# A long convolution by a two-stage transform: the spectral product as three real products, formed per k1 from PSUM and written in place

## Chip, cores, metric

The kernel runs on one core of one Trainium2 chip. The metric is the device time of one execution in microseconds (us). Engines: PE (TensorE) with its weight loads (PEld), DVE (VectorE), ACT (ScalarE), POOL (GpSimd), SP (SyncE, which issues most DMAs).

## What is computed

```python
def _A_ref(q, k, v, shift_k, ssm_k, ssm_D):          # S = 2048, D = 512
    ...
    for t in range(ks):                              # ks = 4
        k_shift = k_shift + k_pad[:, t:t + S, :] * shift_k[:, ks - 1 - t][None, None, :]
    kv = k_shift * v
    ...                                              # transforms of length 2S of kv and ssm_k, zero padded
    y_f = kv_f * kf_f[None, :, :, :]
    y = irfft(y_f)[:S]
    y = y + kv * ssm_D[None, None, :]
    return q * y
...
h = x + _A_ref(_layernorm(x, axis=-1), A_k, A_v, A_shift_k, A_ssm_k, A_ssm_D)
h2 = h + relu(_layernorm(h, axis=-1) @ w1) @ w2      # Dff = 1376
```

All inputs and the output are bf16. The lines on the transform are shortened here: y is the causal convolution of kv with ssm_k along the 2048 tokens, channel by channel.

## The kernel before

The convolution is computed by matmuls at odd frequencies, each transform split in two stages: 32 values k1 by 64, over n1 (32) and n2 (64) tokens. The program is written in an order by hand and kept in it: each engine runs its instructions in the order of the source, and waits only where data, a tile's buffer or a PSUM bank calls for it. The stages, in order:

1. **Loads and tables.** `sk` (ssm_k), then k and v transposed by DMA, on SP's queue. DVE and POOL make turn tables, ACT makes sines of them: f1hi and f1lo for stage 1, cc, cs, cn (`table`, L183; negation on POOL, L204) for stage 2, each with the sine doubled to two halves of 64 columns.
2. **Rows of ssm_k** (`to_rows`, L220): 64 PE transposes of bf16 128x128, eight copies of 128x1024 out of PSUM, in turn by DVE and ACT.
3. **Stage 1 of ssm_k and the taps** (loop at L281): per group gb, `stage1` is 64 matmuls of 32 rows, four row groups at a time, into two PSUM tiles of two banks, each emptied by one copy (L213 on ACT, L215 on DVE) to a1k. `taps` (L272) makes half a chunk of k_shift by eight matmuls of 512 columns, and DVE multiplies it with vT (L279). PSUM: four buffers of two banks.
4. **Rows of kv** (L291), then **stage 2 of ssm_k** (L298): 128 matmuls of 256 columns; DVE writes the real part plus ssm_D to kf, ACT the imaginary part.
5. **Stage 1 of kv** (L311) to a1x.
6. **Product** (L328 and L346, loop at L364): per pair of k1, eight stage 2 matmuls of kv to the tiles u; ACT copies 80 of 256 columns to usb for POOL; DVE and POOL form all four real products (L341); two pairs later PE adds them by ipos and ineg (four matmuls of 512 columns, L351), and ACT copies the sums over kf. The loads of x (first half) and w1 start in this loop.
7. **Inverse stage 1** (`inv1`, L474): per batch of four groups eight matmuls of 256 columns with kf as weights and dre, dim moving, then one copy of 128x1024 to ax. Between the batches stand the layernorm of x, the tables ecore (ec_turns on POOL, ec_wrap on DVE, ec_sins on ACT; two work buffers ecw), and the centring of w1.
8. **Inverse stage 2, gate and MLP** (`inv2`, `gate`, `mlp1`, `mlp2`) over four quarters of the tokens; output by DMA.

Of the kernel before, what the change touches and what calls it, by code (L numbers as in the profile page):

```python
# [9 lines left out]
ALU = mybir.AluOpType  # L10
# [5 lines left out]
P = 128  # L16
# [40 lines left out]
def kernel(  # L57
# [28 lines left out]
    slotA = pl.push("slotA")  # L86
    vp = pl.push("vp")
    early = pl.push("early")
    wp = pl.push("wp", side="right")
    kvp = pl.push("kvp", side="right")  # L90
    psum = pl.push("psF", bufs=4, space=PSUM)


    sk = early.tile([P, DC, S], BF16, name="sk")
    nc.sync.dma_start(out=sk[:], in_=A_ssm_k.rearrange("(c p) t -> p c t", p=P))
    wsh = consts.tile([P, DC, KS], BF16, name="wsh")
    nc.scalar.dma_start(out=wsh[:], in_=A_shift_k.rearrange("(r p) j -> p r j", p=P))
    dtab = consts.tile([P, 64, DC], BF16, name="dtab")
    draw = consts.tile([P, DC, 64], BF16, name="draw")
    for dp in range(2):  # L100
        src = bass.AP(tensor=A_ssm_D.tensor, offset=A_ssm_D.offset + 64 * dp, ap=[[0, 64], [P, DC], [1, 64]])
        nc.scalar.dma_start(out=draw[64 * dp:64 * dp + 64, :, :], in_=src)
    vT = vp.tile([P, DC, S], BF16, name="vT")
    CH = 512
    kT = [(kvp if c < 2 else early).tile([P, DC, CH + 16], BF16, name=f"kT{c}") for c in range(4)]
    wdiag = kvp.tile([P, DC, KS, P], BF16, name="wdiag")
# [9 lines left out]

# [5 lines left out]
    eps_t = consts.tile([P, 1], F32, name="eps_t")  # L122
    nc.vector.memset(eps_t[:], EPS)

    hsc = consts.tile([P, 2], F32, name="hsc")
    hbi = consts.tile([P, 2], F32, name="hbi")
    for t_, v_ in ((hsc, TURN / 8192), (hbi, -0.5 * TURN)):
        nc.vector.memset(t_[:], 0.0)
        for dp in range(2):
            nc.vector.memset(t_[halves[dp], dp:dp + 1], v_)  # L130
# [6 lines left out]
    n1i = early.tile([P, 1], I32, name="n1i")  # L137
    for s in range(0, P, 32):
        nc.gpsimd.iota(n1i[s:s + 32, :], pattern=[[0, 1]], base=0, channel_multiplier=1)
    r1 = early.tile([P, 32], I32, name="f1_r")  # L140
    nc.gpsimd.iota(r1[:], pattern=[[2, 32]], base=1, channel_multiplier=0)
    n2i = early.tile([P, 1], I32, name="n2i")
    for s in range(0, P, 64):
        nc.gpsimd.iota(n2i[s:s + 64, :], pattern=[[0, 1]], base=0, channel_multiplier=1)
    r2 = early.tile([P, 32, 64], I32, name="w_r")
    nc.gpsimd.iota(r2[:], pattern=[[2, 32], [128, 64]], base=1, channel_multiplier=0)
    r3 = early.tile([P, 64], I32, name="dm_r")
    nc.gpsimd.iota(r3[:], pattern=[[1, 64]], base=0, channel_multiplier=0)
    ident = consts.tile([P, P], BF16, name="ident")
    nc.gpsimd.memset(ident[:], 0.0)  # L150
    nc.gpsimd.affine_select(out=ident[:], in_=ident[:], compare_op=ALU.not_equal, fill=1.0,
                            base=0, pattern=[[-1, P]], channel_multiplier=1)

    n1c = early.tile([P, 1], F32, name="n1c")
    n2c = early.tile([P, 1], F32, name="n2c")
# [3 lines left out]
    t1 = early.tile([P, 64], I32, name="f1_t")  # L159
    _turns(nc, t1[:, 0:32], r1[:], n1c[:], 128, True)  # L160
    _turns(nc, t1[:, 32:64], r1[:], n1c[:], 128, False)
    f1f = early.tile([P, 64], F32, name="f1_f")
# [4 lines left out]
    def pieces(name, *sizes):  # L167
        got, at = [], 0
        for i, n in enumerate(sizes):
            got.append((at, wp.tile([P, n, P], F32R, tag=f"{name}{i}", name=f"{name}{i}")))  # L170
            at += n
        return got

    cc, cs, cn = pieces("c2c", 16, 16), pieces("c2s", 22, 10), pieces("c2n", 8, 8, 8, 8)

    def at_k1(tab, k1):
        a, t = [p for p in tab if p[0] <= k1][-1]
        return t[:, k1 - a, :]

    tsn = early.tile([P, 32, 64], I32, name="w_ts")  # L180
    _turns(nc, tsn[:], r2[:], n2c[:], 8192, False)

    def table(dst, turns):  # L183
        for a, t in dst:
            for dp in range(2):
                nc.scalar.activation(out=t[:, :, 64 * dp:64 * dp + 64], in_=turns[:, a:a + t.shape[1], :], func=ACT.Sin,  # L186
                                     scale=hsc[:, dp:dp + 1], bias=hbi[:, dp:dp + 1])

    table(cs, tsn)
    f1hi = consts.tile([P, P], BF16, name="f1_hi")  # L190
    f1lo = consts.tile([P, P], BF16, name="f1_lo")
    for f in (f1hi, f1lo):
        nc.gpsimd.memset(f[:, 64:128], 0.0)
    nc.vector.tensor_copy(out=f1hi[:, 0:64], in_=f1f[:])
    f1d = early.tile([P, 64], F32, name="f1_d")
    nc.vector.tensor_tensor(out=f1d[:], in0=f1f[:], in1=f1hi[:, 0:64], op=ALU.subtract)
    nc.vector.tensor_copy(out=f1lo[:, 0:64], in_=f1d[:])
    _turns(nc, r2[:], r2[:], n2c[:], 8192, True)
# [3 lines left out]
    for a, b in ((0, 8), (8, 16), (16, 22), (22, 24), (24, 32)):  # L202
        (ao, to), (ai, ti) = [[p for p in tab if p[0] <= a][-1] for tab in (cn, cs)]
        nc.gpsimd.tensor_single_scalar(out=to[:, a - ao:b - ao, :], in_=ti[:, a - ai:b - ai, :].bitcast(F32), scalar=-1.0,  # L204
                                       op=ALU.mult)


    nc.gpsimd.tensor_copy(out=dtab[:], in_=draw[:].rearrange("p r g -> p g r"))

# [7 lines left out]
    def bank2(name):  # L217
        return psum.tile([P, 2, 512], F32, tag="ps", name=name)

    def to_rows(src, q, fl, eng):  # L220
        pst = psum.tile([P, 2, 8, P], BF16, tag="ps", name="pst")
        for i in range(8):
            nc.tensor.transpose(out=pst[:, 0, i, :], in_=src[:, :, :, 8 * q + i], identity=ident[:])  # L223
        copy(eng, fl[:, :, :, 8 * q:8 * q + 8], pst[:, 0, :, :].rearrange("p i (d g) -> p g d i", d=2))

    def stage1(fl, a_out, gb, engs, wide=False):

        pss = [bank2("ps1") for _ in range(2)]
        outs = [pss[rg // 2][:, rg % 2, :] for rg in range(4)]
        for gi in range(8):  # L230
            for f, first in ((f1hi, True), (f1lo, False)):
                for rg in range(4):
                    rows = slice(32 * rg, 32 * rg + 32)
                    w = 128 if wide and gi < 7 else 64
                    nc.tensor.matmul(out=outs[rg][:, 64 * gi:64 * gi + w],  # L235
                                     lhsT=fl[rows, 8 * gb + gi, :, :].rearrange("p d n -> p (d n)"),
                                     rhs=f[rows, 0:w], start=first, stop=not first,
                                     tile_position=(32 * rg, 0), skip_group_check=True)
        for h in range(2):
            copy(engs[h], a_out[:, :, 32 * gb:32 * gb + 32].rearrange("p c (g r) -> p c g r", r=DC)[:, :, :, 2 * h:2 * h + 2],  # L240
                 pss[h][:].rearrange("p r (g c) -> p c g r", c=64))

    def stage2(ps, a_in, kp, s):

        for kk in range(2):
            k1 = 2 * kp + kk
            w_re, w_im = ((cc, cs), (cn, cc))[s]
            nc.tensor.matmul(out=ps[:, kk, :], lhsT=at_k1(w_re, k1), rhs=a_in[:, k1, :], start=True, stop=False,  # L248
                             skip_group_check=True)
            nc.tensor.matmul(out=ps[:, kk, :], lhsT=at_k1(w_im, k1), rhs=a_in[:, 32 + k1, :], start=False, stop=True,  # L250
                             skip_group_check=True)
# [393 lines left out]
```

## Time and profile before

| | us |
|---|---|
| median of 3 runs | 229.88 |
| lowest, highest | 229.82, 231.06 |
| span of the profiled execution, first to last instruction | 230.8 |

The span of the profiled execution is 0.9 us above the median of the runs, and inside their lowest and highest.

| engine | busy us | share of the span |
|---|---|---|
| PE | 201.4 | 87% |
| PEld | 142.4 | 62% |
| DVE | 142.9 | 62% |
| ACT | 118.1 | 51% |
| POOL | 78.3 | 34% |

A line of the groups gives the source line, the engine, the operation, what it writes from what, the shape written and read, and the count; then busy us, mean ns of one; then the idle time of that engine before it and what ended it. A line of the waits reads "who, on which line <- for whom: us in total, times, longest". A line by stretch gives the busy us of PE, PEld, DVE, ACT and POOL with their counts, then the granted share of PE's clock, the DMA share and GB/s. Matmuls are pipelined, so the duration of one is longer than the distance between the starts of two.

### The profile page before, as it was taken

The numbers are of one execution on the slowest core, as the hardware profiler recorded it, in microseconds if no ns is written. First come the engines' busy times: TensorE is split into PE (matmuls) and PEld (weight loads), VectorE is DVE, ScalarE is ACT, GpSimd is POOL, SyncE is SP. The second block draws the span as 40 slices with busy tenths as digits, with TensorE's granted clock in tenths as the row PEclk, the third lists the DMA queues.
The fourth block names the chain that finished last, engine by engine and source line by source line (L and its number), as shares of the span: only waits on it lengthen the run. The fifth ranks groups of instructions, "written<-read, shape, count | busy, mean of one in ns | idle before, by whom it ended". The sixth has DMA issues, their size and how long they took to land.

```text
span 230.8 us, 5978 instructions
## 1 busy us (share of the span) xinstructions
PE 201.4 (87%) x2544; PEld 142.4 (62%) x2544; DVE 142.9 (62%) x214; ACT 118.1 (51%) x177; POOL 78.3 (34%) x108
## 2 busy tenths in 40 slices
PE   0485999899966699999898889999999999999991
PEld 0473454899955699998787775444744474444440
DVE  7974667676664589998685869583971346134031
ACT  3789766555585478888486501750162026206400
POOL 6399910000000599998860770400220002002000
PEclk9999999999999589999999997999999999999998
DMA  6999920000000000772962168977244214021011
GB/s 197 306 230 161 169 60 3 0 4 0 0 7 6 3 1 0 182 244 77 211 119 53 33 214 127 213 140 114 54 91 96 55 37 91 6 59 27 3 46 46
DMA packets 49194, 20.10 MB, mean 87 GB/s; under 512 B 44208, under 2 KB 47632, under 8 KB 49168
## 3 DMA queue, kind: packets, MB, share of 16 engines
q1 hardware_dynamic: 46688, 18.24, 37.7%
q10 hardware_dynamic: 2480, 1.48, 2.4%
q8 instruction: 20, 0.33, 0.6%
q14 instruction: 6, 0.05, 0.1%
HBM read 7.08 MB, written 2.10 MB: 40 GB/s over the span
## 4 chain that ended last, share of the span: by engine, by line
PE 78%; ACT 8%; DMA 4%; DVE 4%; POOL 3%; issue 2%; POOLq 0%
PE ps1m L552 17%; PE ps2m L565 16%; PE pz L540 7%; PE psy L351 6%; PE pst L223 5%; PE pkv L276 5%; PE u L248 4%; PE u L250 4%; DMA sk<-in_A_ssm_k_dram 4%; PE ps2k L248 3%; PE ps2k L250 3%; PE ps L235 3%; ACT a1x L213 3%; PE psi L479 2%; ACT c2c L186 2%
## 5 line engine op out<-in xcount | busy, mean ns | idle before, releaser
L554 ACT ACTIVATE h1T<-ps1m 128x512 bf16<-128x512 f32 (+1 forms) x44 | 26.0, 596 | 57.6 <-PE ps1m L552 57.6
L552 PE MATMUL ps1m<-xT,w 128*128 128x512 bf16 (+1 forms) x176 | 40.3, 390 | 0.0
L565 PE MATMUL ps2m<-w,h1T 128*128 128x512 bf16 (+1 forms) x176 | 38.7, 379 | 0.0
L568 DVE SCALAR_TENSOR_TENSOR o<-ps2m,rstd,xh 128x512 bf16<-128x512 f32 x16 | 12.0, 750 | 38.8 <-PE ps2m L565 38.7
L552 PEld LDWEIGHTS <-w 128*128 128x128 bf16 (+1 forms) x176 | 17.8, 102 | 21.1 <-issue 2.2
L341 DVE TENSOR_TENSOR t<-u,kf 128x704 fp32r<-128x704 f32 x32 | 27.1, 888 | 5.3 <-ACT usb L337 5.3
L341 POOL TENSOR_TENSOR t<-usb,kf 128x320 fp32r<-128x320 f32 x32 | 28.6, 923 | 4.2 <-ACT usb L337 3.2
L565 PEld LDWEIGHTS <-h1T 128*128 128x128 bf16 (+1 forms) x176 | 17.2, 98 | 20.7
L429 POOL TENSOR_SCALAR rstd<-mv 128x4 f32<-128x4 f32 x8 | 1.9, 241 | 66.4 <-DVE mv L427 66.3
L425 DVE BATCH_NORM_STATS2 st<-xh 128x6 f32<-128x512 bf16 x32 | 19.7, 676 | 0.0
L213 ACT CAST kf<-psy 128x512 fp32r<-128x512 f32 x30 | 17.5, 643 | 1.8 <-PE psy L351 0.2
L540 PE MATMUL pz<-ecore,ax 32*128 32x256 f32 (+7 forms) x512 | 15.7, 274 | 2.1 <-ACT ax L213 1.1
L540 PEld LDWEIGHTS pz<-ecore,ax 32*128 32x128 f32 x512 | 15.2, 185 | 3.4 <-issue 2.1
L276 PE MATMUL pkv<-kT,wdiag 128*128 128x512 bf16 x64 | 15.2, 380 | 1.6 <-POOL c2n L204 1.2
L479 PE MATMUL psi<-dre,kf 128*128 128x256 f32 x64 | 16.0, 290 | 0.4 <-ACT ax L213 0.4
L351 PE MATMUL psy<-t,ipos 128*128 128x512 f32 x48 | 15.8, 390 | 0.0
L321 POOL CAST ipos<-ident 128x128 fp32r<-128x128 bf16 x1 | 0.3, 289 | 45.5 <-ACT a1x L213 45.5
L213 ACT CAST a1k<-ps 128x1024 fp32r<-128x1024 f32 x13 | 13.0, 1068 | 5.4 <-PE ps L235 5.4
L279 DVE TENSOR_TENSOR vT<-pkv,vT 128x1024 bf16<-128x1024 f32 x8 | 9.8, 1225 | 9.4 <-PE pkv L276 9.2
L479 PE MATMUL psi<-dim,kf 128*128 128x256 f32 x64 | 15.5, 283 | 0.0
L213 ACT CAST ax<-psi 128x1024 fp32r<-128x1024 f32 x12 | 11.7, 1012 | 7.3 <-PE psi L479 4.3
L223 PE MATMUL pst<-ident,sk 128*128 128x128 bf16 x64 | 6.7, 293 | 9.2 <-DMA sk<-in_A_ssm_k_dram 9.2
(110 smaller groups left out, 410.9 us busy)
## 6 DMA issues: line engine op xcount, KB each, us to landing
sk<-in_A_ssm_k_dram SPq DMA_DIRECT2D x1, 2048.0 KB, 8.5
xh<-in_A_q_dram SPq DMA_DIRECT2D x16, 128.0 KB, 3.2
out_dram<-o SPq DMA_DIRECT2D x64, 32.0 KB, 1.6
w<-in_B_w_dram SPq DMA_DIRECT2D x1, 1376.0 KB, 6.0
w<-in_B_w_dram ACTq DMA_DIRECT2D x1, 1280.0 KB, 6.5
w<-in_B_w_dram ACTq DMA_DIRECT2D x1, 96.0 KB, 6.3
draw<-in_A_ssm_D_dram ACTq DMA_DIRECT2D x2, 32.0 KB, 8.4
kT<-in_A_k_dram SPq DMA_TRANSPOSE x4, 6.8
```

The costliest lines, as they stand in the source:

```text
L213: nc.scalar.copy(out=o, in_=i)
L223: nc.tensor.transpose(out=pst[:, 0, i, :], in_=src[:, :, :, 8 * q + i], identity=ident[:])
L248: nc.tensor.matmul(out=ps[:, kk, :], lhsT=at_k1(w_re, k1), rhs=a_in[:, k1, :], start=True, stop=False, skip_group_check=True)
L276: nc.tensor.matmul(out=ps[:, i, :], lhsT=wdiag[:, 2 * h + i, j, :], rhs=kT[c][:, 2 * h + i, 16 - j:CH + 16 - j], start=(j == 0), stop=(j = ...
L341: eng.tensor_tensor(out=t[:, :, j, :], in0=in0.unsqueeze(1).to_broadcast([P, 2, n, 2]), in1=kfr[:, :, j, ks], op=ALU.mult)
L351: nc.tensor.matmul(out=psy[:], lhsT=m_[:], rhs=t_.rearrange("p j k -> p (j k)"), start=first, stop=not first)
L425: nc.vector.bn_stats(out=st[:, i, :], in_=src[:, i, :])
L479: nc.tensor.matmul(out=ps[:, i // 2, i % 2, :], lhsT=kf[:, c, 4 * m:4 * m + 4, :].rearrange("p r k -> p (r k)"), rhs=d[:].rearrange("p d a ...
L540: nc.tensor.matmul(out=pz[:, rg, j:j + w, :].rearrange("p a b -> p (a b)"), lhsT=ax[rows, 64 * rho + n2, :, :].rearrange("p d g -> p (d g) ...
L552: nc.tensor.matmul(out=ps1[:fsz, :].rearrange("p (i t) -> p i t", i=4), lhsT=w1[:, c, fc * P:fc * P + fsz], rhs=hT[sc][:, :, c, :], start= ...
L554: nc.scalar.activation(out=h1T[:fsz, fc, :], in_=ps1[:fsz, :], func=ACT.Relu)
L565: nc.tensor.matmul(out=ps2[:], lhsT=h1T[:ksz, fc, i * P:(i + 1) * P], rhs=w2[:ksz, fc, :], start=(fc == 0), stop=(fc == NFC - 1))
```

## The change

Every second stage is merged into one loop, and the tables, rows and buffers around it are changed to suit:

- **Tables.** One table st per k1 with sine, cosine and negated sine (64 columns each) replaces cc, cs and cn; POOL makes from it sm, the difference and the sum of cosine and sine on a block diagonal.
- **Rows as words.** `to_rows` moves two bf16 as one f32 word: 32 transposes in place of 64 per tensor, two PSUM tiles of four banks, each emptied half by ACT and half by DVE.
- **Stage 1.** One PSUM tile of four banks per group, two buffers in all; one engine reads one half of each bank, the other the other half. For ssm_k DVE adds dmask, which holds ssm_D, and ACT copies. `taps` runs every second group and covers a whole chunk in four banks.
- **Product.** Per two k1 three units: `pairs` for each k1 (eight 64-row matmuls: ssm_k and kv, both halves) and `sums` for both (eight full matmuls). ACT copies the part of ssm_k to kt, DVE multiplies the part of kv by it and writes the result over BK (pairs) or the first half of BX (sums). POOL and the adding matmuls have no part in it.
- **Inverse stage 1** takes BK and BX as weights, with three matmuls per group (256, 128, 128 columns), and writes two tiles ax by two copies per batch.
- **Buffers.** x (first half) is loaded after the product; w2, the MLP's tiles, x (second half), xT and three of qT lie in the space of BK, and so are filled after inverse stage 1. One work buffer ecw in place of two.

```diff
-    psum = pl.push("psF", bufs=4, space=PSUM)
+    psum = pl.push("psF", bufs=2, space=PSUM)
+    BK = bkp.tile([P, 2, DC, 32, 64], F32R, tag="K", name="BK")
...
+    st = stp.tile([P, 32, 192], F32R, name="st")
+    sm = smp.tile([P, 2, 32, P], F32R, name="sm")
+    _sin(st[:, :, 0:64], tsn, 8192)
...
+    nc.gpsimd.tensor_single_scalar(out=st[:, :, 128:192], in_=st[:, :, 0:64].bitcast(F32), scalar=-1.0, op=ALU.mult)
...
+    def bank4(name, dt=F32):
+        return psum.tile([P, 4, 512], dt, tag="ps", name=name)
+    def to_rows(src, h, fl):
+        pst = bank4("pst").rearrange("p b (i c) -> p (b i) c", i=4)
...
+        for i in range(16):
+            nc.tensor.transpose(out=pst[:, i, :], in_=srcw[:, :, 16 * h + i], identity=identw[:])
+        w = 16 * h
+        nc.scalar.copy(out=flw.bitcast(F32)[:, :, w:w + 8], in_=pst[:, 0:8, :].rearrange("p i c -> p c i"))
+        nc.vector.tensor_single_scalar(out=flw[:, :, w + 8:w + 16],
+                                       in_=pst[:, 8:16, :].bitcast(I32).rearrange("p i c -> p c i"),
+                                       scalar=0, op=ALU.bitwise_or)
+    def stage1(fl, B, gb, dmul=None):
+        ps = bank4("ps1")
...
+        pv = ps.rearrange("p r (g h c) -> p h r c g", h=2, c=32)
+        if dmul is not None:
+            nc.vector.tensor_tensor(out=B[:, 0, :, :, gs], in0=pv[:, 0],
+                                    in1=dmul[:, :, gs].unsqueeze(2).to_broadcast([P, DC, 32, 8]), op=ALU.add)
+            nc.scalar.copy(out=B[:, 1, :, :, gs], in_=pv[:, 1])
+        else:
+            nc.scalar.copy(out=B[:, 0, :, :, gs], in_=pv[:, 0])
+            nc.vector.tensor_copy(out=B[:, 1, :, :, gs], in_=pv[:, 1])
...
     for gb in range(8):
-        stage1(kfl, a1k, gb, "AD" if gb in (2, 4, 6) else "AA")
-        taps(gb // 2, gb % 2)
+        stage1(kfl, BK, gb, dmask)
+        if gb % 2 == 1:
+            taps(gb // 2)
...
+    def forms(ps):
+        kt = prod.tile([P, 2, 256], F32, tag="kt", name="kt", bufs=3)
+        nc.scalar.copy(out=kt[:], in_=ps[:, :, 0:256])
+        return kt
+    def pairs(k1):
+        ps = psum.tile([P, 2, 512], F32, tag="u", name="u")
+        for x, B in enumerate((BK, BX)):
+            for i, t in ((0, st[:, k1, 64:192]), (1, st[:, k1, 0:128])):
+                for dp, pq in enumerate(halves):
+                    nc.tensor.matmul(out=ps[:, dp, 256 * x:256 * x + 256], lhsT=t[pq], rhs=B[pq, i, :, k1, :],
+                                     start=(i == 0), stop=(i == 1), tile_position=(64 * dp, 0), skip_group_check=True)
+        return ps, forms(ps), BK[:, :, :, k1, :]
+    def sums(k1):
+        ps = psum.tile([P, 2, 512], F32, tag="u", name="us")
+        for x, B in enumerate((BK, BX)):
+            for j in range(2):
+                for i in range(2):
+                    nc.tensor.matmul(out=ps[:, j, 256 * x:256 * x + 256], lhsT=sm[:, i, k1 + j, :], rhs=B[:, i, :, k1 + j, :],
+                                     start=(i == 0), stop=(i == 1), skip_group_check=True)
+        return ps, forms(ps), BX[:, 0, :, k1:k1 + 2, :].rearrange("p r k g -> p k r g")
+    def times(unit):
+        ps, kt, o = unit
+        nc.vector.tensor_tensor(out=o, in0=ps[:, :, 256:512].rearrange("p s (r g) -> p s r g", r=DC),
+                                in1=kt[:].rearrange("p s (r g) -> p s r g", r=DC), op=ALU.mult)
+    for k1 in range(0, 32, 2):
+        units = [pairs(k1), pairs(k1 + 1), sums(k1)]
+        for u in units:
+            times(u)
...
     def inv1(b):
...
+            nc.tensor.matmul(out=ps[:, i].rearrange("p d a n -> p (d a n)"), lhsT=BX[:, 0, :, :, g].rearrange("p r k -> p (r k)"),
+                             rhs=inv3[:].rearrange("p d a n -> p (d a n)"), start=True, stop=False, skip_group_check=True)
+            for dp in range(2):
+                nc.tensor.matmul(out=ps[:, i, dp].rearrange("p a n -> p (a n)"),
+                                 lhsT=BK[:, dp, :, :, g].rearrange("p r k -> p (r k)"),
+                                 rhs=inv12[:].rearrange("p a n -> p (a n)"), start=False, stop=True, skip_group_check=True)
+        for rho in range(2):
+            copy("D" if rho == 1 and b % 2 == 1 else "A", ax[rho][:, :, 4 * b:4 * b + 4, :],
+                 ps[:, :, :, rho, :].rearrange("p i d n -> p n i d"))
...
         if b == 4:
             ec_sins(0)
-            ec_turns(2)
             center(nc.vector, 0, cen[0][:, 0:FS])
+            ec_turns(1)
             ec_wrap(1)
...
+    M = bkp.tile([P, 32768], BF16, tag="K", name="M")
...
+    lift(0)
+    load_x(2)
+    load_x(3)
+    lift(1)
+    ec_turns(2)
```

## The prediction, made before the changed kernel was run

> **What bounds the kernel now.** I read the chain of waits first: 78% of it is PE, so the kernel is a row of stages, each limited by PE or by the hand-over between PE and the engines that empty PSUM. Then I read the busy time of each engine by stage, with bounds taken from the chain.
>
> ```profile
> 21.70:41.20 19.50, 16.83 (x441) 8.54 (x441) 11.97 (x10) 12.93 (x14) 7.58 (x14) 1.00 0.46 78
> 47.20:62.40 15.20, 15.20 (x128) 15.09 (x126) 10.48 (x9) 7.33 (x8) 0.00 (x0) 1.00 0.01 2
> 62.40:77.00 14.60, 8.78 (x514) 7.40 (x513) 7.57 (x7) 11.08 (x11) 0.79 (x2) 0.95 0.02 5
> 77.00:84.00 7.00, 7.00 (x35) 6.83 (x36) 5.12 (x6) 2.84 (x9) 5.23 (x6) 0.63 0.01 2
> 84.00:109.80 25.80, 25.73 (x159) 22.71 (x157) 22.68 (x27) 22.43 (x55) 23.41 (x26) 1.00 0.39 115
> 109.80:131.40 21.60, 18.29 (x148) 17.12 (x148) 15.65 (x27) 14.18 (x17) 12.14 (x20) 1.00 0.51 100
> ```
>
> Columns: stretch and length, busy time of PE, PEld, DVE, ACT, POOL, then granted clock. In order: stage 1 of ssm_k with the taps; stage 2 of ssm_k (PE full); stage 1 of kv (PE 60%, waits for copies); stage 2 of kv with the product, at clock 0.63 first and then PE full; inverse stage 1. What follows 131.4 is left nearly as it is by the change.
>
> Next the prices, from the groups by shape, and one line of the waits.
>
> ```profile
> L341 DVE TENSOR_TENSOR t<-u,kf 128x704 fp32r<-128x704 f32 x32 | 27.1, 888 | 5.3 <-ACT usb L337 5.3
> L279 DVE TENSOR_TENSOR vT<-pkv,vT 128x1024 bf16<-128x1024 f32 x8 | 9.8, 1225 | 9.4 <-PE pkv L276 9.2
> L523 DVE TENSOR_TENSOR qT<-pz,qT 128x2048 bf16<-128x2048 f32 x4 | 9.1, 2286 | 5.2 <-PE pz L540 3.1 <-issue 2.1
> L308 ACT CAST kf<-ps2k 128x1024 fp32r<-128x1024 f32 x8 | 8.1, 1014 | 8.0 <-PE ps2k L250 8.0
> L554 ACT ACTIVATE h1T<-ps1m 128x512 bf16<-128x512 f32 x40 | 23.8, 597 | 56.8 <-PE ps1m L552 56.8
> ```
> ```profile
> DVE t L341 <- ACT usb L337: 5.3, 14, 2.5
> ```
>
> Two things to see. DVE reading PSUM costs 1.05 ns an element plus about 0.15 us: 704, 1024, 2048 elements take 888, 1225, 2286 ns, so 512 take about 0.70. And DVE's product waits for ACT's copy usb, which it does not read. Both read the same PSUM tile u: its two readers go one after the other.
>
> Last, the clock, in stretches of 3.4 us:
>
> ```profile
> 72.10:75.50 3.40, 1.54 (x105) 1.35 (x100) 1.19 (x2) 1.76 (x3) 0.43 (x2) 0.99 0.02 5
> 75.50:78.90 3.40, 1.94 (x9) 1.94 (x10) 0.94 (x2) 1.70 (x3) 0.63 (x2) 0.50 0.00 0
> 78.90:82.40 3.50, 3.50 (x18) 3.50 (x18) 3.48 (x5) 1.17 (x4) 3.50 (x5) 0.52 0.02 5
> 20.90:24.30 3.40, 2.15 (x70) 1.24 (x69) 0.00 (x0) 3.40 (x5) 3.40 (x3) 1.00 1.30 172
> ```
>
> A stretch with 1.54 us of PE work is followed by half clock, and a half-clock stretch with 1.94 us by another; one with 2.15 is not. At half clock the u matmuls start every 0.21 us instead of 0.12.
>
> **The sum, stage by stage.** It is made against the profiled span, 230.8 us. That is 0.9 over the median 229.88, so the difference found is added to the median.
>
> *Rows and stage 1 of ssm_k.* sk still lands at 9.2. 32 word transposes replace 64. The trace has no f32 transpose: 0.083 us (the quick pace of the bf16 ones) and 0.227 (an f32 psy matmul, four times as wide) bound it. I take 0.11, nearest to the bf16 rows, 3.5 us in all. With the last copy (1.23) the rows are ready at 14.0, not 16.9. DVE's four dm_t instructions (2.15 in the trace) come next, to 16.2. ACT's shorter sines and POOL's dmask (wdiag ends at 14.1, then some 1.6) are done by then.
>
> Here the cost begins. PSUM now holds two tiles of four banks, where there were four of two. Each stage 1 tile is read by both DVE (1.23) and ACT (1.02), so one after the other, where two separate tiles were emptied side by side. One taps product on DVE now covers 2048 elements, 2.29. Tiles alternate: the next taps need the tile of the stage 1 group issued before them, whose DVE copy stands in DVE's queue behind the previous taps product. So the ring is taps product 2.29, DVE copy 1.23, ACT copy 1.02, taps 16 x 0.216 + 0.2 = 3.66, and four hand-overs of about 0.04: 8.35 us for two groups, against 4.9 before (two of 2.45 in the chain). First taps product ends 16.2 + 1.23 + 1.02 + 3.7 + 2.29 + 0.2 = 24.6; three rounds more give 49.7. Before: 41.1. **+8.6.**
>
> In each round PE has 3.5 us of taps and then about 5 us with only two groups (0.55 each) in it, so a 3.4 us stretch with under 1.5 us of work falls into every round. Half clock on all taps would cost 4 x 3.5 = 13.8; none costs 0. Stretches and taps do not line up, so I take some 3 us of half clock per taps, 1.5 lost each: **+6**. The row speaks for it more than the page does. The Trainium skill, "TensorE: Matmul & The Clock Gate", "HAM oscillation", warns only of PE idle beyond about 3.4 us. No single pause here is longer than 2 us, so by the page this term would be 0; in the trace the clock fell with pauses of 1.4 and 2.3 us.
>
> *Rows of kv.* Before 41.1 to 48.4, 7.3. After: 32 transposes (3.5) with the last copy (1.25), and 0.4 for the slow clock: 5.2. **-2.1.** If the new row tile, which stands where kT stood, must wait for POOL's table work, POOL is free only at 48 to 55 (from 15.8: negation 5.4, two memsets about 3, four sums of 2048 elements at 2.06 to 2.9 ns from the w and t rows, small ones 4): 0 to 3 us. I take 0, for it ends about when the taps do.
>
> *Stage 2 of ssm_k* is no stage any more: 48.3 to 62.4, **-14.1**.
>
> *Stage 1 of kv.* Each tile: PE 0.75, ACT 1.05, DVE 1.23, hand-overs, about 3.2 for two tiles; eight tiles with fill 13.9, and 1.2 for half clock, against 14.6. **+0.5.**
>
> *Product.* Per two k1: three units, each an ACT copy of 512 (0.60) and one DVE product of 512 (0.70). PE: pairs are 64-row matmuls; the 32-row ones at L540 start four within 8 ns, 117 ns a group, so I take the two halves side by side: 4 x 0.117 = 0.47 for a pair unit, 8 x 0.117 = 0.94 for sums, 1.88 in all. DVE 2.09, ACT 1.8. The first product writes BK over what sums reads, so it waits for two matmuls of sums; DVE is still on the previous round's third product then. So DVE bounds: 48 x 0.70 = 33.6, fill 2.4, half clock at the start 1.5: 37.5, against 33.5 (77.0 to 110.5). **+4.0.** POOL's 28.6 us of products and 64 wide psy matmuls go, but POOL's share ran beside PE; DVE now does all of it.
>
> *Inverse stage 1.* 192 matmuls (64 of 256 columns, 128 of 128) replace 128 of 256, which start every 0.120. Halving the columns saves little: in the pz groups 64 to 224 columns take 92 to 109 ns, 256 take 117, as if the weight load set the pace. At 0.112: 21.5 against 15.4. Around it: column sums first, 1.25 after the last product, and 1.2 later; last copies 1.3. One buffer ecw makes DVE's ec_wrap(1) wait for POOL's turns (2.1), which wait for ACT's sines (1.45); behind ec_wrap(1) on DVE stands a copy whose PSUM tile PE needs: 2.4 lost. Together 27.7 against 20.9. **+6.8.** The x loads now start after the product; eight issues of 0.45 and 3.2 to landing put xh0 about 2 us into this stage, and their statistics end just before PE wants the tile behind them; 3 us later would cost 1.5.
>
> *Rest.* The lifts (4.7 to landing) move behind inverse stage 1, with eight x loads between them on SP's queue. inv2(0) and the first half of gate (4.0 + 2.3) cover the first lift; without that cover it would cost up to 4.7. **0.**
>
> Sum: 8.6 + 6 - 2.1 - 14.1 + 0.5 + 4.0 + 6.8 = **+9.7**, so 229.88 + 9.7 = **239.6 us**.
>
> **Rivals.**
> - *The clock stays up.* The k loop of before kept 1.00 with pauses of 1.4 us. Without the terms 6, 0.4, 1.2 and 1.5 the sum is +0.6: 230.5. Against it: 5 us with 1.1 us of work.
> - *Faster: the two readers of a stage 1 tile run side by side*, as the two tiles of before do at 25.4 and 25.8. Then the ring is 7.2 (1.02 less in each of four rounds, with hand-overs 4.5), stage 1 of kv is DVE's 9.8 + 1.1 (3.0 less), and the pause between taps is 3.6 us with 1.1 of work, so the clock holds (6 + 0.4 + 1.2): -5.4, 224.5. With the slow clock as forecast it gives +2.2, 232.1: it decides only where the pause falls so far that the clock stays. The usb wait speaks against it.
> - *TensorE dearer.* Word transposes at 0.227: 64 x 0.117 = +7.5. Halves one after the other: a round of PE 2.82 against 2.09, 16 x 0.73 = +11.7. Either gives 247 to 251, both 259.
> - *The change does not do what it says*, a product still with its own stage 2: the diff leaves no such loop; no chance given.
>
> **How the numbers follow.** Forecast 0.52 (232 to 247, from its open terms: clock 0 to 14, POOL 0 to 3, loads 0 to 1.5, inverse pace 0.105 to 0.120, which is -1.3 to +1.5); clock up 0.11; side by side 0.17; TensorE dearer 0.20. A measurement tells about 0.5% (1.15 us) from no change: faster 0.17, same 0.10 (most of the clock case), slower 0.73. The range leaves out under one in ten on either side: from 226, short of the full faster case, to 253, past either dearer price alone. The forecast's own is 232 to 247.
>
> **What would show it.** Right: taps products about 8 to 10 us apart, ACT's stage 1 copy starting when DVE's ends; clock near 0.5 in parts of that loop; product rounds of 2.1 us with DVE full; inverse stage 1 at 0.11 us a matmul with DVE stopped once before ec_wrap(1). Wrong: DVE and ACT reading one tile at once; taps at 0.216 throughout; product rounds of 2.6 or more set by PE or by the wait on BK; transposes at 0.2.

## The result and the profile after

Median 276.83 us (275.76 to 277.47, 4 runs) against 230.47 (229.82 to 233.64, 4 runs): the ratio is 1.201, 95% interval 1.195 to 1.207. The forecast was 239.6 with a range of 226 to 253. The sign was right; the size, 46 us instead of 10, was not. One of the four runs before, 233.64, lies 1.7% above the fastest; the median of the other three is 229.88, which makes the ratio 1.204.

The profiled execution took 275.76 and spans 274.0, 43.2 more than before. First by stretch (the columns as before): tables held up; stage 1 of ssm_k with the taps; stage 1 of kv; the product in its two clocks; inverse stage 1; the rest. The rows of kv, 64.8 to 71.1, are left out.

```profile
16.70:29.20 12.50, 1.24 (x128) 1.23 (x129) 11.08 (x7) 1.99 (x4) 12.40 (x4) 0.60 1.02 184
29.20:64.80 35.60, 23.12 (x444) 10.85 (x447) 15.91 (x10) 6.96 (x7) 20.43 (x15) 0.85 0.00 1
71.10:86.30 15.20, 7.75 (x512) 6.63 (x512) 9.59 (x9) 8.00 (x8) 0.00 (x0) 0.59 0.09 16
86.30:91.00 4.70, 4.69 (x30) 4.25 (x32) 1.29 (x2) 1.75 (x3) 0.00 (x0) 0.51 0.65 262
91.00:126.40 35.40, 34.02 (x358) 29.91 (x354) 29.96 (x46) 24.93 (x46) 0.00 (x0) 1.00 0.01 2
126.40:173.60 47.20, 45.49 (x208) 44.34 (x208) 14.76 (x29) 15.75 (x28) 14.34 (x20) 0.63 0.15 34
173.60:274.00 100.40, 94.21 (x860) 52.20 (x864) 49.56 (x96) 28.24 (x48) 11.21 (x17) 0.96 0.54 104
```

In the first line PE works 1.2 of 12.5 us while DVE is busy for 11.1 and POOL for 12.4. In the sixth the weight loads are busy for 44.3 of 47.2 us. These two stretches hold most of what the forecast missed. Set against the forecast's own lengths (us; half clock put where it was forecast):

| stretch | forecast | measured | missed |
|---|---|---|---|
| rows of ssm_k ready | 14.0 | 16.7 | +2.7 |
| from there to the end of the first taps product | 12.1 | 20.2 | +8.1 |
| three more rounds of the loop | 29.6 | 27.9 | -1.7 |
| rows of kv | 5.2 | 6.3 | +1.1 |
| stage 1 of kv | 15.1 | 15.2 | +0.1 |
| product | 37.5 | 40.1 | +2.6 |
| inverse stage 1 | 27.7 | 47.2 | +19.5 |
| rest | 99.4 | 100.4 | +1.0 |

Then the groups that answer to those priced, and one line of the waits. The last two groups are the weight loads of inverse stage 1 in the kernel before.

```profile
L439 PE MATMUL psi<-inv,BK 128*128 128x128 f32 x128 | 34.7, 367 | 0.0
L439 PEld LDWEIGHTS psi<-inv,BK 128*128 128x128 f32 x128 | 34.4, 316 | 0.0
L321 DVE TENSOR_TENSOR BK<-u,kt 128x512 fp32r<-128x512 f32 x32 | 20.6, 686 | 8.3 <-PE us L315 8.3
L249 DVE TENSOR_TENSOR E<-pkv,E 128x2048 bf16<-128x2048 f32 x4 | 9.2, 2292 | 21.0 <-PE pkv L246 21.0
L479 PEld LDWEIGHTS psi<-dim,kf 128*128 128x128 f32 x64 | 12.3, 192 | 0.0
L479 PEld LDWEIGHTS psi<-dre,kf 128*128 128x128 f32 x64 | 12.2, 191 | 0.7 <-ACT ax L213 0.6
```
```profile
ACT BK L227 <- DVE BK L225: 23.5, 3, 8.0
```

DVE's two prices came out as taken (0.69 and 2.29). In the product DVE now waits for PE, 8.3 us, where it was to be full. ACT's stage 1 copy waits for DVE's copy of the same tile: two readers go in sequence. And a weight load of inverse stage 1 lasts 316 ns, where one of before, for the same 128 x 128 f32, lasted 191 to 192.

### The profile page after: what moved, and what is told of

The parts are those of the page before. It is cut to its first block, busy times and chain, and to the rows that moved or that the text cites. A ratio compares the mean times of both kernels' runs of the same rounds, so it can differ in the third digit from the quotient of the medians.

```text
span 274.0 us, 6020 instructions
## 1 busy us (share of the span) xinstructions
PE 219.7 (80%) x2600; PEld 158.3 (58%) x2608; DVE 145.3 (53%) x216; ACT 96.8 (35%) x150; POOL 70.4 (26%) x79
## 4 chain that ended last, share of the span: by engine, by line
PE 57%; issue 29%; DVE 7%; DMA 3%; ACT 2%; POOL 0%
PE ps1m L529 14%; PE ps2m L542 14%; PE psi L439 8%; PE psi L436 7%; PE pz L517 7%; PE pkv L246 4%; DMA E<-in_A_ssm_k_dram 3%; PE pst L204 2%; DVE BK L225 2%; DVE E L249 2%; DVE dm_t L44 2%; DVE dm_t L46 1%; PE pm L416 1%; ACT BK L227 1%; DVE E L207 0%
## 5 line engine op out<-in xcount | busy, mean ns | idle before, releaser
L531 ACT ACTIVATE M<-ps1m 128x512 bf16<-128x512 f32 (+1 forms) x44 | 25.9, 595 | 59.1 <-PE ps1m L529 59.1
L529 PE MATMUL ps1m<-M,w 128*128 128x512 bf16 (+1 forms) x176 | 38.8, 379 | 1.1 <-issue 1.1
L542 PE MATMUL ps2m<-M 128*128 128x512 bf16 (+1 forms) x172 | 38.5, 379 | 0.2
L439 PE MATMUL psi<-inv,BK 128*128 128x128 f32 x128 | 34.7, 367 | 0.0
L439 PEld LDWEIGHTS psi<-inv,BK 128*128 128x128 f32 x128 | 34.4, 316 | 0.0
L436 PE MATMUL psi<-inv,BX 128*128 128x256 f32 x64 | 32.6, 510 | 0.0
L246 PE MATMUL pkv<-kT,E 128*128 128x512 bf16 x60 | 19.2, 478 | 16.1 <-ACT BK L227 15.7
L542 PEld LDWEIGHTS <-M 128*128 128x128 bf16 (+1 forms) x176 | 17.2, 98 | 20.8
L321 DVE TENSOR_TENSOR BK<-u,kt 128x512 fp32r<-128x512 f32 x32 | 20.6, 686 | 8.3 <-PE us L315 8.3
L436 PEld LDWEIGHTS psi<-inv,BX 128*128 128x128 f32 x64 | 20.0, 313 | 0.2
L257 POOL TENSOR_TENSOR sm<-st 64x2048 fp32r<-64x2048 f32 x4 | 18.0, 4510 | 0.2
```

The costliest lines, as they stand in the source:

```text
L246: nc.tensor.matmul(out=ps[:, i, :], lhsT=wdiag[:, i, j, :], rhs=kT[c][:, i, 16 - j:CH + 16 - j], start=(j == 0), stop=(j == KS - 1))
L257: nc.gpsimd.tensor_tensor(out=sm[pq, i, :, 64 * dp:64 * dp + 64], in0=st[pq, :, 64:128].bitcast(F32), in1=st[pq, :, 0:64].bitcast(F32), op=op)
L321: nc.vector.tensor_tensor(out=o, in0=ps[:, :, 256:512].rearrange("p s (r g) -> p s r g", r=DC), in1=kt[:].rearrange("p s (r g) -> p s r g" ...
L436: nc.tensor.matmul(out=ps[:, i].rearrange("p d a n -> p (d a n)"), lhsT=BX[:, 0, :, :, g].rearrange("p r k -> p (r k)"), rhs=inv3[:].rearr ...
L439: nc.tensor.matmul(out=ps[:, i, dp].rearrange("p a n -> p (a n)"), lhsT=BK[:, dp, :, :, g].rearrange("p r k -> p (r k)"), rhs=inv12[:].rea ...
L529: nc.tensor.matmul(out=ps1[:fsz, :].rearrange("p (i t) -> p i t", i=4), lhsT=w1[:, c, fc * P:fc * P + fsz], rhs=hT[sc][:, :, c, :], start= ...
```

## The experiments

Differences are between profiled spans (274.0 after). All but run 8 are single runs, on three chips, where the kernel before took 229.38, 231.76 (the median of seven runs) and 232.69; so a difference of totals below some 3 us shows nothing by itself, and the stages of the trace have to show it.

**1. Inverse stage 1 with neighbouring weights.** A word is 4 bytes, one f32 or f32r value.

```diff
-  lhsT=BX[:, 0, :, :, g].rearrange("p r k -> p (r k)"),
+  lhsT=BX[:, 0].rearrange("p r k g -> p (r k g)")[:, 128 * g:128 * g + 128],
-      lhsT=BK[:, dp, :, :, g].rearrange("p r k -> p (r k)"),
+      lhsT=BK[:, dp].rearrange("p r k g -> p (r k g)")[:, 128 * g:128 * g + 128],
```

> Leaves the right columns out: the weights of inverse stage 1 are read from 128 neighbouring words in place of 128 words 64 apart, so the sums it makes are others; every count, shape and wait is as in the changed kernel. Theory STEP (the weight load of 128 words 64 apart takes about 0.22 us, and three of them make the 0.67 us a group): a group falls to about 3 x 0.115 = 0.35, inverse stage 1 from 47.2 to about 28, the total by 18 to 20 us, to about 256. Theory NARROW (f32 matmuls of 128 columns run at a quarter of the pace, 0.21 each, whatever the weights): no change, 276. Theory CLOCK (half clock, 131.8 to 155.7 and 162.6 to 179.6, doubles the matmuls): no change by this edit.

Measured: 261.94 us, span 260.2 (-13.8). Twelve matmuls take 1.36 us instead of 2.66, inverse stage 1 takes 29.6 instead of 47.2 (-17.6); the rest takes 3.8 more, part of it at half clock (10.2 us from 162.7 on, against 6.0). The groups of this run:

```profile
L439 PE MATMUL psi<-inv,BK 128*128 128x128 f32 x128 | 22.1, 255 | 0.0
L439 PEld LDWEIGHTS psi<-inv,BK 128*128 128x128 f32 x128 | 20.6, 198 | 0.0
```

Same shapes, same counts, only other addresses: 316 becomes 198. The number of columns was not to blame. Nor was the clock: in the changed kernel the first batches, up to 131.8, run at clock 1.00 and take 2.66 like those at half clock. At half clock neighbours are hardly cheaper: the one such batch of run 1 takes 2.46 from its first start to its last, where the others take 1.25 to 1.31 and batches 64 apart 2.43 to 2.53. So the step costs what half clock costs, and does not add to it.

**2. Which steps are dear.** Each of the 16 batches of twelve matmuls reads its weights with a step of its own.

```diff
+  STEP = (64, 1, 2, 4, 8, 16, 32, 64, 63, 65 - 3, 60, 48, 40, 24, 12, 3)
...
+  lhsT=BX[:, 0].rearrange("p r k g -> p (r k g)")[:, 0:127 * n + 1:n],
```

> Leaves the right columns out as well: each of the 16 batches of inverse stage 1 reads its weights with another step between the 128 words: 64, 1, 2, 4, 8, 16, 32, 64, 63, 62, 60, 48, 40, 24, 12, 3. Theory STEP: the time of a batch (12 matmuls, 2.67 us at step 64) falls to about 1.4 at step 1 and shows from which step the load is dear; if it is a matter of powers of two, 63, 62, 60 are as cheap as 1; if it is a matter of distance, they cost what 64 costs. Theories NARROW and CLOCK: 2.7 us in all batches, but for waits.

Measured: 276.95 us. The clock changes within the stage, so the batches have to be read in two sets. The batches of steps 1, 2, 4 and 3 (columns as before):

```profile
131.60:133.00 1.40, 1.40 (x14) 1.40 (x14) 0.93 (x2) 1.08 (x2) 0.00 (x0) 1.00 0.87 202
133.00:134.40 1.40, 1.40 (x14) 1.40 (x14) 1.40 (x3) 0.59 (x1) 0.00 (x0) 1.00 0.05 12
134.40:137.20 2.80, 2.80 (x14) 2.80 (x14) 1.67 (x8) 1.07 (x2) 1.65 (x2) 1.00 0.00 0
170.80:173.40 2.60, 2.60 (x13) 2.60 (x13) 0.00 (x0) 1.07 (x2) 0.00 (x0) 0.50 0.00 0
```

From the first start to the last in a batch, in us. At clock 1.00: step 1 1.25, step 2 1.30, step 4 2.57, step 8 2.66, step 48 2.42, step 60 2.57, step 64 2.47. At clock 0.50: step 3 2.35, 32 and 64 2.44 to 2.45, 63 2.56, 24 2.77, 12 2.93, 40 3.52 (16 and 62 fall across a change of the clock). At full clock the price doubles between a step of 2 words (8 bytes) and of 4 (16 bytes), and powers of two are no worse than others. Step 3 shows nothing on this: its 2.35 is what a step of 2 words takes at half clock (run 7). Why 12, 24 and 40 cost more than 64 is not known. The Trainium skill, "Advanced Engine Details and Errata", "SBUF Cachelines", says that SBUF is read in lines of 16 bytes and that at least two accesses must fall on a line to hide its latency; steps of 2 and of 4 words agree with that. This sentence spoke against the change, and the prediction did not use it.

**3. dm_t earlier.** The four DVE instructions of dm_t are moved to just behind the big turn tables.

```diff
     _turns(nc, r2, r2, n2c[:], 8192, True)
+    t3 = kvp.tile([P, 2, 64], I32, name="dm_t")
+    _turns(nc, t3[:, 0, :], r3[:], n2c[:], 64, True)
+    _turns(nc, t3[:, 1, :], r3[:], n2c[:], 64, False)
```

> The result stays whole: the four small dm_t instructions of DVE (64 integers each, 4.2 and 3.4 us on the trace of the changed kernel, under 1 in that of before) stand before the row copies, while POOL runs its short wdiag products. Theory POOL (each waits until POOL's running instruction ends: negation 5.4 us, two memsets 3.5 us): they take about 0.2 to 1 us each, the first stage 1 copy starts at about 17 and not 24.5, the first taps at about 20 and not 29.2, total 8 to 10 us less, about 267. Rival (the instructions are slow in themselves, or DVE waits for ACT's sine): they stay at 3 to 4 us or another wait takes their place, total within 2 us of 276.8.

Measured: 268.79, span 267.0 (-7.0); the last taps product ends at 56.8 instead of 64.8. The timelines, first DVE and POOL of the changed kernel (start, length):

```profile
16.63 4.17 DVE L44 TENSOR_SCALAR dm_t<-dm_r,n2c 128x64 int32<-128x64 int32 x1
20.84 3.46 DVE L46 TENSOR_SCALAR dm_t<-dm_t 128x64 int32<-128x64 int32 x1
20.95 3.39 DVE L44 TENSOR_SCALAR dm_t<-dm_r,n2c 128x64 int32<-128x64 int32 x1
24.37 3.47 DVE L46 TENSOR_SCALAR dm_t<-dm_t 128x64 int32<-128x64 int32 x1
24.48 3.37 DVE L225 TENSOR_TENSOR BK<-ps,dmask 128x1024 fp32r<-128x1024 f32 x2
```
```profile
15.36 5.40 POOL L187 TENSOR_SCALAR st<-st 128x2048 fp32r<-128x2048 f32 x1
20.71 7.08 POOL L254 MEMSET sm<- 64x4096 f32 x2
27.86 4.51 POOL L257 TENSOR_TENSOR sm<-st 64x2048 fp32r<-64x2048 f32 x1
```

Here each DVE instruction ends when POOL's does: 20.8 with the negation, 24.3 and 27.8 with the two memsets (3.5 each). The copy of the first stage 1 tile stands behind them. With dm_t early, POOL is at its four wdiag products instead:

```profile
10.13 1.03 DVE L44 TENSOR_SCALAR dm_t<-dm_r,n2c 128x64 int32<-128x64 int32 x1
11.20 0.96 DVE L46 TENSOR_SCALAR dm_t<-dm_t 128x64 int32<-128x64 int32 x1
12.08 1.08 DVE L44 TENSOR_SCALAR dm_t<-dm_r,n2c 128x64 int32<-128x64 int32 x1
13.20 1.21 DVE L46 TENSOR_SCALAR dm_t<-dm_t 128x64 int32<-128x64 int32 x1
```

They are held still, but by instructions of 1.04 us. So in these two kernels the length of POOL's running instruction holds DVE. It is no rule without exception. In the kernel before:

```profile
16.34 0.75 DVE L44 TENSOR_SCALAR dm_t<-dm_r,n2c 128x64 int32<-128x64 int32 x1
17.12 0.97 DVE L46 TENSOR_SCALAR dm_t<-dm_t 128x64 int32<-128x64 int32 x1
18.01 0.24 DVE L44 TENSOR_SCALAR dm_t<-dm_r,n2c 128x64 int32<-128x64 int32 x1
18.29 0.20 DVE L46 TENSOR_SCALAR dm_t<-dm_t 128x64 int32<-128x64 int32 x1
14.22 5.55 POOL L204 TENSOR_SCALAR c2n<-c2s 128x1024 fp32r<-128x1024 f32 x2
```

The first ends with the first of POOL's two negations (17.04); the other three run beside the second (to 19.77) and do not wait for its end. Why those three pass is not known. The Trainium skill, "SBUF — State Buffer", "Who interferes with whom", says that DVE and GpSimd share a pair of ports, held for a whole instruction by whoever comes first, and that a tensor_scalar on DVE can be of the kind that needs it; the timelines of the changed kernel and of this run agree, and so does DVE's PSUM copy at 36.95 to 38.09, which ran its usual length beside POOL; the last three lines of DVE in the kernel before do not.

**4. The other layout.** BK and BX with g outermost: weights are neighbours, but what the product reads and DVE writes is 32 words apart.

```diff
-    BK = bkp.tile([P, 2, DC, 32, 64], F32R, tag="K", name="BK")
+    BK = bkp.tile([P, 2, 64, DC, 32], F32R, tag="K", name="BK")
```

> The result stays whole: BK and BX are laid out with the group g outermost and k1 innermost, so weights of inverse stage 1 are 128 neighbouring words, and the moving operands and results of the product are 32 words apart. Theory STEP for weights alone: inverse stage 1 about 28, product as it is (rounds of 2.3 us), total about 257. If moving words 32 apart are as dear as weights 64 apart: a product round goes from 2.29 to about 4 us (16 x 1.7 = +27), and DVE's strided results may add; total about 284. NARROW or CLOCK: no gain in inverse stage 1, total 277 or more.

Measured: 289.69, span 287.9 (+13.9). Twelve matmuls of inverse stage 1 take 1.36, but product matmuls start every 0.218 instead of 0.118 at full clock, and the product takes 63.6. The dear step only moved from the weights to the moving operand and DVE. DVE's product instructions take 1.0 to 1.85 us instead of 0.69 and DVE is busy for 58.2 of the 63.6, PE for 62.5; which of the two sets the length was not separated.

**5. The ring of the loop.** On top of the early dm_t: four tiles of two banks, one reader each, half a chunk of taps per group; ssm_D is folded into sk. Only the buffers and the loop are shown of this edit.

```diff
-    psum = pl.push("psF", bufs=2, space=PSUM)
+    psum = pl.push("psF", bufs=4, space=PSUM)
...
-        stage1(kfl, BK, gb, dmask)
-        if gb % 2 == 1:
-            taps(gb // 2)
+        stage1(kfl, BK, gb, "AD" if gb in (2, 4, 6) else "AA")
+        taps(gb // 2, gb % 2)
```

> Edit on top of the early dm_t of the run before: the k loop as it was, with one reader for each PSUM tile (two tiles of two banks per group of stage 1, four of them in the ring, ssm_D folded into the kernel's first row instead of the diagonal added in the copy). RING (the tile that both engines read in sequence and the two buffers of four banks set the rounds of 9.86 us): the four rounds fall to what TensorE and VectorE need each, the last taps product ends at about 38 us instead of 56.8, the rows and stage 1 of kv gain up to 2 us more, the total is about 249 (18 to 20 below the kernel with dm_t early, 268.8). Rival CLOCK (TensorE at half clock sets the rounds): the last taps product ends at 52 to 57, the total stays within 4 us of 268.8.

Measured: 253.67, span 251.9 (-15.1 against the early dm_t). First the ring in the changed kernel, from the chain (pieces of 0.05 us or less are left out):

```profile
34.66 2.29 DVE E L249
36.95 1.14 DVE BK L225
38.11 1.02 ACT BK L227
39.17 0.38 PE pkv L246
39.60 4.89 PE pkv L246 x14
44.52 2.29 DVE E L249
```

9.86 us from one taps product to the next, in just the order that the forecast gave, with the taps at 5.3 for half clock in place of 3.66. Without it, the whole loop:

```profile
22.00:43.00 21.00, 19.70 (x576) 10.23 (x576) 13.31 (x14) 14.33 (x28) 20.72 (x6) 1.00 0.42 75
```

PE is busy for 19.7 of 21.0 us, at clock 1.00, and the eight groups take 21.0 us instead of some 40; the last taps product ends at 43.1, not at the hoped-for 38. This takes away two readers, two buffers and half clock together; which part each has is not separated. The rest of the hoped-for 18 to 20 went to this edit's own costs: the fold of ssm_D stands behind dm_t and the transposes start at 14.3 instead of 9.1, and the copies of kv's rows wait for POOL until 49.2.

**6. No change of row mode.** Each pair of 64-row matmuls side by side becomes one of 128 rows: as many slots, no change between 64 and 128 rows, and no adding of two products into one.

```diff
-  for dp, pq in enumerate(halves):
-      nc.tensor.matmul(out=ps[:, dp, ...], lhsT=t[pq], rhs=B[pq, i, :, k1, :], ...
+  nc.tensor.matmul(out=ps[:, i, ...], lhsT=t, rhs=B[:, i, :, k1, :], ...
```

> Edit: each pair of half products (two times 64 rows side by side) becomes one product over all 128 rows, four instead of eight slots of the same length, so that TensorE's time for the matmuls is the same and it never changes between 64 and 128 rows; this leaves the split of the two halves out of the product. Everything else as in the changed kernel (276.8). SWITCH (each change between 64-row and 128-row matmuls costs TensorE about 0.2 us, twice a round): the rounds of the product fall from 2.29 to 2.1, where VectorE's three instructions of 0.688 become the bound; product 34 to 37 us instead of 40.1, total 273 to 274. Rival PACE (the matmuls themselves, or the hand-over of the PSUM tile, set 2.29): rounds stay at 2.25 to 2.3, total within 1 us of the changed kernel.

Measured: 270.82, span 269.1 (-4.9); rounds of 1.95 instead of 2.29, product 33.4 instead of 40.1. First PE in the changed kernel, from sums (128 rows) to pairs (64 rows):

```profile
118.89 0.40 PE L306 MATMUL u<-BX,st 64*128 64x256 f32 x4
119.22 0.74 PE L315 MATMUL us<-BK,sm 128*128 128x256 f32 x4
119.80 0.64 PE L315 MATMUL us<-BX,sm 128*128 128x256 f32 x4
120.36 0.51 PE L306 MATMUL u<-BK,st 64*128 64x256 f32 x4
120.71 0.40 PE L306 MATMUL u<-BX,st 64*128 64x256 f32 x4
```

The first sums matmul starts 0.205 after the last pair, the second 0.223 after the first, then 0.117 to 0.121 each; the same at the change back. Two gaps of some 0.2 where 0.118 would do, twice a round, are about 0.4 us. In this run every start is 0.116 to 0.121 after the last, but for one a round of 0.16 to 0.17. The product gains 6.7 us, the whole only 4.9; the stages behind it take 1.8 more. The rounds even went under 2.06, three times DVE's 0.69: neighbouring DVE instructions overlap in the trace, so the bound by DVE (2.09) was itself at least 0.14 too high.

**7 and 8. Pairs of groups side by side.** Weights 2 words apart, and the product's operands in runs of 2 words: first alone (without ssm_D), then with the early dm_t and the loop of run 5.

```diff
-    BK = bkp.tile([P, 2, DC, 32, 64], F32R, tag="K", name="BK")
+    BK = bkp.tile([P, 2, 32, DC, 32, 2], F32R, tag="K", name="BK")
```

> Edit: the two word buffers keep two neighbouring groups g beside each other, so that weights of inverse stage 1 are read 2 words apart (64 in the changed kernel) and the product's moving operands and writes go in runs of 2 words; the copy of the first chunk goes in without ssm_D, which leaves the D term out. STEP (a step of weights up to 2 words is read at full pace, and runs of 2 words are too): inverse stage 1 takes 28 to 31 us instead of 47.2, rounds of the product stay at 2.29 (40 us), total 258 to 263. Rival RUNS (a run of only 2 words costs what single words 32 apart cost: 0.22 for a matmul, 1.43 for VectorE's instruction): inverse stage 1 28 to 31, product 60 to 80, total 275 to 295.

> Edit: early dm_t, the k loop with one reader for each PSUM tile, and the pairs of groups, all three, with ssm_D folded into the kernel's first row. If the three causes are separate and their sizes add (8 for dm_t, 18 to 20 for the ring, 17 for the weights' step): 276.8 - 8 - 19 - 17 = 233, range 228 to 240, so about the kernel before (230.5) with no sure sign. Rival OVERLAP (what one frees is lost again to the clock or to another wait): 241 to 255. If runs of 2 words are dear: over 255.

Measured: 314.83, and 285.11 to 291.72 in four runs (1.24 times the kernel before, 95% interval 1.224 to 1.257), so run 8 ends where its third case, dear runs, had it: over 255. Both theories of the first missed part: the product did become dear, but beyond the price given, for the clock stayed down. The stretch of the product in run 7:

```profile
87.80:170.40 82.60, 82.59 (x384) 70.70 (x384) 45.04 (x47) 28.17 (x47) 0.00 (x0) 0.50 0.04 15
```

PE is marked busy without a gap for 82 us and yet is granted half its clock to the end, with 0.287 between starts where the changed kernel has 0.213 at half clock. In run 8 the clock came back within 5 us of the product's end, and the weights 2 words apart were cheap: inverse stage 1 took 30.8. In run 7 the clock stayed down well beyond the product:

```profile
170.40:198.40 28.00, 26.29 (x121) 24.94 (x121) 12.47 (x24) 10.54 (x19) 6.73 (x15) 0.50 0.25 57
```

These are matmuls of inverse stage 1, whose moving operands are neighbours, at the 0.213 of half clock.

**9. What keeps the clock down.** Run 7, with moving operands from neighbouring words (in the sums too, not shown), and DVE's writes in runs of 2 words as they were.

```diff
-  rhs=B[pq, i, :, :, k1].rearrange("p g r e -> p (g r) e"),
+  rhs=BX[pq, 1].rearrange("p g r k e -> p (g r k e)")[:, 256 * k1:256 * k1 + 256],
```

> Edit on the kernel with pairs of groups (product 80 us, clock 0.5 through all of it, 0.287 between matmuls): the product's moving operands come from 256 neighbouring words of the image's second half, which nothing writes there; VectorE's products are still written in runs of 2 words. This leaves the right columns out of the product. READS (moving operands in runs of 2 words make a matmul 0.287 at half clock, and TensorE, which then works for only 0.213 of 0.287, does not get its clock back): 0.213 between matmuls at first, the clock at 1.0 within 10 us of the product's start, 0.118 from then on, rounds set by VectorE or TensorE at 2.3 to 3.5, product 40 to 60 us, total 275 to 295. Rival CLOCK (the clock stays down for another reason, and 0.287 is its price): clock 0.5 throughout the product with 0.21 or more between matmuls, product over 65 us, total over 300. VectorE's instruction of 1.62 (every other one of the pairs): 0.69 if it met TensorE's reads in runs, unchanged if its own writes make it.

Measured: 259.84, span 258.0; both the total and the product came out below the ranges of READS.

```profile
85.40:124.20 38.80, 38.80 (x384) 34.27 (x384) 30.58 (x47) 26.12 (x47) 0.00 (x0) 0.94 0.09 33
125.50:155.90 30.40, 26.92 (x208) 25.76 (x208) 14.73 (x30) 15.64 (x28) 11.87 (x17) 0.94 0.24 53
```

The clock is back within some 5 us and the product takes 38.8. So within the product the reads in runs of 2 words cost both: 35% a matmul at half clock, and the clock. Whether the length of the run, the 64 words between runs or the finer pattern itself makes a matmul dear was not separated. DVE's writes cost nothing by themselves: 0.69 again, where run 7 had 1.62 in every other one of the pairs. Why the clock stays down is open. That PE's array works for too little of each 0.287 is argued, not shown, and two rows speak against it: in run 4 product matmuls 0.218 apart, where 0.118 would do, kept clock 1.00 from 91.4 to the end of the product at 150.2, and in run 7 the clock stayed at 0.50 for 28 us after such reads had ended. The rule of two accesses to a line, quoted at run 2, would have let such runs pass; the measurement decides.

**10. All four suspects away.** The edits of 1, 3, 5 and 6 together.

> Edit: the four suspects taken away together: dm_t early, the k loop with one reader for each PSUM tile, one full product in place of each pair of halves, weights of inverse stage 1 from 128 neighbouring words (the last two leave the split of the halves and the right columns out). ADD (the four are separate and nothing else is left): from the runs with one each, dm_t -8, ring -15, change of row mode -6, weights -17 to -18 (the half of the half clock after it counted in): 276.8 - 46 to 47 = 230 to 231, within 4 us of that, so the kernel before's 230.5 is met. Rival OVERLAP (what one gives is in part the others', or another wait comes up behind): 238 to 250. The product 33 us, inverse stage 1 27 to 30, last taps product at about 42.

Measured: 233.78, span 232.0, with 229.38 for the kernel before on the same chip.

```profile
22.00:43.00 21.00, 19.74 (x576) 10.15 (x574) 13.00 (x14) 14.22 (x28) 20.72 (x6) 1.00 0.47 70
65.10:98.90 33.80, 33.80 (x256) 33.63 (x256) 29.89 (x46) 24.84 (x47) 0.00 (x0) 0.92 0.12 42
100.30:129.90 29.60, 26.23 (x208) 24.93 (x208) 14.65 (x29) 15.63 (x28) 11.61 (x17) 0.94 0.25 56
```

Loop, product and inverse stage 1. One by one the four gave 13.8 + 7.0 + 15.1 + 4.9 = 40.8; together 42.0. They are separate and they add, as nearly as single runs on different chips can show; that the two sums agree to 1.2 us is partly luck. Against the kernel before 4.4 us are left.

**11. Do transposes pay for the step?** The rows' transposes read weights 32 words apart at 0.112, which does not fit run 2. The 192 products become 192 transposes of the same words, 64 apart.

```diff
+  nc.tensor.transpose(out=ps[:, i, dp].rearrange("p a n -> p (a n)"),
+                      in_=BK[:, dp, :, :, g].bitcast(F32).rearrange("p r k -> p (r k)"), identity=identw[:])
```

> Edit on the changed kernel: the 192 products of inverse stage 1 become 192 transposes of the same 128 x 128 words, 64 apart, against the identity (this leaves inverse stage 1 out). The transposes of the rows read words 32 apart and took 0.112 each at full clock, the products of inverse stage 1 0.222. STEP (any load of 32-bit weights from words 4 or more apart takes 0.22): twelve transposes take 2.67 us, the stage 47, total 277. FORM (only the product's weights pay for the step, a transpose's do not): twelve take 1.35 at full clock and 2.56 at half, the stage 27 to 33, total 256 to 264.

Measured: 265.74, span 263.9.

```profile
L439 PEld LDWEIGHTS psi<-identw,BK 128*128 128x128 f32 x128 | 26.0, 261 | 0.0
```

0.147 from start to start at clock 1.00, a load of 261 ns: between the two theories. A transpose pays a third on 0.112, a product double. Why they differ stays open.

No kernel that computes the reference beat the one before: the best, run 5, takes 253.67 against 229.40 to 234.26 in seven runs of the kernel before on its chip. A layout in which both the weights and the product's operands are neighbours was not found; each word is read once along k1 and once along g.

## Why the prediction was wrong

- **Inverse stage 1, "At 0.112: 21.5", is the step that failed** (+19.5). That the weight load sets the pace was right; its price was not. The pace came from rows of before whose weights all lie side by side: the pz groups, and inverse stage 1 as it was. The diff has them 64 words apart (`BX[:, 0, :, :, g]`), and that was never compared. Measured: 0.222 a matmul, at full and at half clock alike (a group of three takes 0.665 in both), so the 192 take 42.6 us instead of 21.5 and the stage 47.2 instead of 27.7; with neighbouring weights the stage takes 29.6. The range for this pace, -1.3 to +1.5, came from rows that all have neighbouring weights.
- **"DVE's four dm_t instructions (2.15 in the trace)"** failed too (+8.1 up to the end of the first taps product). The moved step kept its old price. POOL's order around it is new: a negation of 5.4 and memsets of 3.5 run just there, and each dm_t instruction ends with one of them, so the four take 11.2. The prediction counted this POOL work, but for another wait. The old row had a hint: two of the four took 0.75 and 0.97, the other two 0.24 and 0.20.
- **Rows of ssm_k** (+2.7): 1.7 is the transposes, which go every 0.213 for the first 3.2 us of PE's work and every 0.112 after. The granted clock reads 1.00 in those 3.2 us, but the trace's first record of the clock, of 1.00, begins only at 12.37, just where the pace changes, so that reading is no measurement. The row of before had the same sign: its first transposes go every 0.107 until 13.96, later ones every 0.085 or so, and its first record of the clock is at 13.98. The other 1.0 is a copy: DVE's last one (`15.49 1.23`) starts when ACT's of the same tile ends, at 15.46. The prediction read that two readers go one after the other, and used it for stage 1 but not here; the **rows of kv** (+1.1) show the same.
- **Product** (+2.6): the mechanism was wrong, and that the size is nearly right is luck. PE sets 2.29, for the changes of row mode, which were put at nothing, and DVE's bound of 2.09 was too high. The Trainium skill, "TensorEngine Tiling (Array Packing)", "Key Properties", says that changing the tiling mode drains TensorE; run 6 agrees: a round with two changes takes 2.29 us, without them 1.95, and the gaps in the trace add up to about 0.4.
- **The ring was right**: rounds of 9.86, 9.86 and 8.17 for 8.35 + 1.5; the two readers in sequence; run 5 takes it away.
- **Half clock on the taps was right**: 5.4, 5.3, 5.3 and 3.6 for 3.66, 5.0 in all for 6. **Stage 1 of kv** was right, 15.2 for 15.1, and the **rest** nearly, +1.0.
- Of the rivals, *TensorE dearer* named the right engine and the wrong places: the halves do run side by side (at most 4 ns apart), and only the first 16 transposes are dear. *Side by side* is refuted by ACT's wait for DVE.

## What to carry to other kernels

When a row is to price a matmul, compare not only shape and type but how its operands lie in SBUF, for weights, moving operand and the engines' writes each; a layout that serves two stages has to be priced in both. When a small instruction is moved, look at what the neighbouring engine runs at that place. And make an unknown's range from rows that differ in the property in question, not from rows that share it.

## What was not expected of the hardware

- At full clock, f32r weights of a product 1 or 2 words apart let a matmul start every 0.113 to 0.119 us, weights 4, 8, 48, 60 or 64 words apart every 0.22 to 0.24 (runs 1, 2 and 8). At half clock neighbours take 0.213 and so do steps of 2 and 3 words, 64 words 0.222, 40 words 0.32. f32 transposes of such weights take 0.112 (32 apart) and 0.147 (64 apart) at full clock.
- Moving operands 32 words apart: 0.218 at full clock (0.118 for neighbours), but hardly a loss at half clock (0.217 against 0.213; run 4). Runs of 2 words, 64 words apart: 0.287 at half clock, and the clock did not come back while they lasted (runs 7 and 8).
- A DVE tensor_scalar on 64 elements took 3.4 to 4.2 us and ended with POOL's memset or tensor_scalar; three of the four in the kernel before ran beside a tensor_scalar of POOL without waiting for its end.
- PE's first transposes go at a slower pace (0.213 against 0.112; in the kernel before 0.107 against some 0.085) for 3.2 us in the changed kernel, 4.7 in the one before and 5.4 in run 5, while the view prints a clock of 1.00; each time the pace changes where the trace's first record of the clock begins (12.37, 13.98, 19.81).
